# A hand-scheduled transformer block on one core: its written-out order replaced by another one

## The chip, the cores and the metric

The kernel runs on one core of a Trainium2 chip. The metric is the device time of one execution in microseconds (us). Five queues of instructions run at once and meet only through semaphores: PE (matmuls and their weight loads), ACT (activations), DVE (vector work), POOL (more vector work) and SP, which here only issues DMAs. Each queue is strictly in order: an instruction that waits holds everything behind it.

## The reference

One sequence of S = 2048 rows of D = 448, in bf16; 16 heads of 28; a gated feed-forward of F = 1792. Cut to what matters:

```python
q, k, v = layernorm(x) @ wqkv                       # 16 heads of 28
pq, pk  = q @ w_phi, k @ w_phi                      # per head, 28 x 28
phi_q   = concat(softmax(pq), softmax(-pq))         # 56 features; phi_k likewise
kv, z   = sum_s phi_k[s] v[s]^T, sum_s phi_k[s]     # over all 2048 rows
o       = (phi_q @ kv) / (phi_q @ z + 1e-6)
h       = x + o @ wo
out     = h + (sigmoid(hn @ w_gate) * (hn @ w_up)) @ w_down     # hn = layernorm(h)
```

The sum over s makes a point that all rows must pass: no output of attention exists before the last row's phi_k is summed.

## The kernel before, in words

The 2048 rows are 16 tiles of 128 (t = 0 to 15). All work is one list of about 1,000 tasks, `K.list`, in `build`. A task names its engine, the tasks it needs, the PSUM banks it may take, and an estimated duration (`dur`), landing time (`lat`) and DMA size. The string `PLAN` (line 31) is the order: each item is a task's number in the list; `.4-7` gives it PSUM banks 4 and 7; `~` moves it to its other engine. `planned` (line 113) reads the string, `emit` (line 147) gives each engine its queue in that order and adds the waits. The estimates are not read there: they served whoever searched the order, and reach the chip only through the string. Tasks with `lock=True` on DVE and the POOL task next to them in the string are made to wait for each other (line 126), so that they don't run at once.

The tasks that matter here, with the line of their instruction:

- **First half, until `kvz`.** Per pair of tiles PE projects k and v (`kp`, `vp`, line 513). Per tile t: two exponentials on ACT into `ek` (`ekp`, `ekm`, line 598; three buffers), the sum of each head on DVE (`ss`, line 611) and its reciprocal (`rs`, line 614), the product `phi` on POOL (line 618; DVE for tiles 12, 14 and 15), v scaled on ACT (`v1`, line 603), and `kv` on PE (line 631), which adds the tile to one PSUM bank. Between these DVE computes the layernorm statistics (`bst`, `agg`, lines 532 and 534) and POOL the factors (`ve`, `pow`, `neg`, lines 540 to 544). `kvz` (DVE, line 695) takes the finished sum.
- **Queries.** `qp` on PE, two exponentials on ACT (line 653), half sums `hs` on POOL (line 667), `sq` and `rq0` on DVE (lines 670, 672), `rq` and `em` on POOL (lines 674, 680; `em` of some tiles on DVE), then a DMA transpose `eT` on SP (line 688).
- **Output of attention, per tile.** `num` on PE (line 704), `rd` and `o` on DVE (lines 712, 714), the transpose `oT` (PE and ACT for tiles 0 and 1, a DMA transpose for each later pair, line 735), `wo_` on PE, `h`, `bst2`, `agg2` on DVE (lines 768 to 773), `ve2`, `pow2`, `nb` on POOL (lines 774 to 787), `hn` on ACT or DVE (lines 783 to 791), and the transpose `hT` (PE for tiles 0 and 1, a DMA transpose after that, line 809).
- **Feed-forward, in five chunks of 2, 4, 4, 4 and 2 tiles.** `gu` (line 513): gate and up products for 14 blocks of columns; each pair of blocks needs four PSUM banks. The chunk's first `gu` needs `hT` of all its tiles. `tg` on ACT (tanh, line 844) and `hh` on DVE (line 851) free the banks. `dn` (line 870) is the down product of one tile, `fin` (line 877) adds it to h, `st` (line 879) stores it. `gu1` below is the chunk of tiles 2 to 5, `gu2` that of tiles 6 to 9, `gu3` of 10 to 13, `gu4` of 14 and 15.
- **Fillers.** `dm` (line 813) multiplies constants and keeps PE busy while it would wait.
- **SP.** All loads, DMA transposes and stores are issued by the one queue SP, in the order of the string.

Of the kernel before, what the change touches and what calls it, by code (L numbers as in the profile page):

```python
# [10 lines left out]
P = 128  # L11
# [20 lines left out]
58 59 60 61 22 661.0-0 67.0-0 20 68 64.1-1 65 69 66 73.2-2 74 70.3-3 75 9 13 15 44 10 62 63 167.4-4 165.5-5 94.6-6  # L32
91.7-7 120 71 72 97.0-0 88.1-1 89 98 95 92 118 121 21 4 119 168~ 5 122 123 124 99~ 96~ 166 90 93 112.2-2 113 125 127
114 128 115 126 169.3-3 171 173 175 170.5-5 76.4-4 172 174 176 193.0-1 177.6-7 180 179 182 77 186 187 183 189 136
190 137 138 132 134 133 139 135 116 129 130 131 184 191 117 140 141 195.2-3 178 78 181 194 196 197 185.4-4 198 188
204 199 205 206 211.5-6 85.0-0 200 82.7-7 212 213.1-2 192 214 83 201 207 86 142 202 208 149 215 216 87 79.3-3
229.0-5 203 84 217 222 224 223 218 150 80 219 143 147 145 144 148 146 209 220 151 152 81 231.1-7 230 234 233 232
247.2-6 240 241 225 226 227 103.3-3 106.0-0 210 221 242 235 248 104 105 249.5-7 109.1-1 107 228 110 100.3-3 101 250
153 251 252 236 156 237 238 243 157 244 254 158 255 160 154 161 155 159 245 102 111 253 108 265.2-3 266 239 319.1-5
258 259 270 269 256 261 262 162 163 263 164 272 277 276 279 273 246 662.0-0 257 320 274 321 322 328 260 327 323 280  # L40
281 267.0-6 283.2-3 284 268 301.1-7 287 288 271 264 335.2-5 302 294 295 278 305 306 329 324 330 331 325 290 297 291
332 292~ 298 326 51 45 46 54 52 334 333 47 336 285.0-3 275 344 345 282 303.1-6 286 304 308 312 313 315 309 316 289
370.5-7 293 299 310~ 307 338 296 314 337 353.0-1 371 354 300 311 379 363 362 380 355 356 373 372 317~ 318 455 346
339 347 421.3-6 461.2-2 456.1-1 422 515.4-4 462 348 463 457 340 458 364 349 350 357 341 365 366 358 464.7-7 387.0-2
519.5-5 459.1-1 465 520 431 460 521 423 430 522 424 342 367 343 352 351 55 516 543 544 545 517 537 546 538 388
404.1-7 518 396 389 390 539 469.6-6 547.5-5 359 470 540 405 541.3-3 466.4-4 397 406 414 407 413 548~ 542~ 663.0-0
701.0-5 702.2-3 703 704 705 707 360 368 361~ 467 471 468 374 381 709.1-6 710.4-7 711 712 375 708 706 715 713 382 716
376 714 383 717.2-3 718.0-5 719 720 721 369 664.4-4 476.4-4 473.7-7 723 722 724 477 474 472 56 725.1-6 726.2-3 727
728 523.0-5 524 478 475 391 398 384 377 385 378 729 731 392 399 393 400 730 733.4-7 734.1-6 735 736 739 737 408 549
732 550 551 409 740 557 479 525.0-2 526 573 558 741.1-3 742.5-6 743 744 386 401 394 395 402 552 425 553 554 415 403  # L50
565 738 559 560 561 562 566 555 747 745 567 568 569 570 749.0-2 750.4-7 751 752 563 753 571 746 748 755 574 483.1-1
438.3-5 480.6-6 575 484 485 754 576 439 481 756 577 578 556 564 572 487.1-1 490.0-0 760.2-2 579~ 491 482 426 488 489
492 580 763.4-7 764.1-6 765 766 447 440 441 448 767 769 761 416 432 433 449 450 451 770 768 410 442 411 486 527.3-5
493 529.0-2 528 530 771.1-6 772.4-7 773 774 605 589 606 581 597 777 775 779.2-5 780.0-3 781 782 598 590 417 607 591
776 582 434 599 778 427 785 786 428 412 452 418 592 783 443 444 583 784 787.1-6 788.4-7 789 790 419 429 435 608 609
# [166 lines left out]
def build(nc, A_x, A_wqkv, A_w_phi, A_wo, B_w_gate, B_w_up, B_w_down, out):  # L222
# [16 lines left out]
    with ExitStack() as es:  # L239
# [67 lines left out]
        def TS(t):  # L307
            return slice(t * P, (t + 1) * P)
# [335 lines left out]
        for u in range(NT // 2):  # L644
# [39 lines left out]
            for a, n in ((t0, 1), (t1, 1)) if u < 2 else ((t0, 2),):  # L684
                for t in range(a, a + n):
                    ET[t] = ("eT", a)
                w = a % NEQ
                task(("eT", a), "sp", 1.25 if n == 1 else 1.9, lambda e, a=a, n=n, w=w: e.dma_start_transpose(
                    out=eqT[:, a:a + n, :, :].rearrange("p t k s -> p (t k) s"),
                    in_=eq[:, w:w + n, :, :].rearrange("p t k s -> p (t k s)")),  # L690
                    [("em", t) for t in range(a, a + n)], lat=1.1, kind="tr", size=1.42 * n)
# [8 lines left out]
        for t in range(NT):  # L700
# [18 lines left out]
            if n == 1:  # L719
                def f(e, t=t):  # L720
                    for k in range(4):
                        r = e.matmul(bank[got(("oP", t))[0]][:, k * P:k * P + P], lhsT=o_pad[:, t % 4, k * P:(k + 1) * P],
                                     rhs=ident[:], start=True, stop=True)
                    return r
                task(("oP", t), "pe", 0.26, f, [("o", t), "ident"], banks=ANY, until=[("oT", t)], mode=128)

                def f(e, t=t):
                    return e.copy(oT[:, t % 4, :, :].rearrange("p g s -> p (g s)"), bank[got(("oP", t))[0]])

                def f2(e, t=t):  # L730
                    return e.tensor_copy(oT[:, t % 4, :, :].rearrange("p g s -> p (g s)"), bank[got(("oP", t))[0]])
                task(("oT", t), "act", 0.53, f, [("oP", t)] + last_read, alt=("dve", 0.6, f2))
            elif t % 2:
                w = slice(t0 % 4, t0 % 4 + 2)
                task(("oT", t0), "sp", 1.25, lambda e, w=w: e.dma_start_transpose(
                    out=oT[:, w, :, :].rearrange("p t g s -> p (t g) s"),
                    in_=o_pad[:, w, :].rearrange("p t k -> p (t k)")),
                    [("o", t0), ("o", t)] + last_read, lat=1.1, kind="tr", size=1.42)
# [27 lines left out]
        for t in range(NT):  # L766
# [40 lines left out]
                task(("hT", t), "act", 0.48, f, [("hP", t)] + read, alt=("dve", 0.6, f2))  # L807
            else:
                task(("hT", t), "sp", 1.25, lambda e, t=t: e.dma_start_transpose(
                    out=hnT[:, :, TS(t)], in_=hn[:, t % NHN, :]), [("hn", t)] + read, lat=1.1, kind="tr", size=0.72)  # L810
# [109 lines left out]
```

## Time and profile before

| | us |
|---|---|
| three runs, median (lowest to highest) | 208.51 (208.28 to 208.68) |
| the profiled execution's own time | 209.01 |
| its span, first to last instruction | 207.3 |
| PE busy | 197.0 (95%) |
| DVE busy | 132.6 (64%) |
| ACT busy | 94.5 (46%) |
| POOL busy | 79.9 (39%) |

The profiled execution took 209.01 us, of which 207.3 us are the span that the profile shows and 1.7 us lie around it. The granted clock of PE is 1.00 over the whole span.

How to read it: a busy PE includes matmuls whose ends are modelled, so small losses between them don't show as idle time. The distance from the start of one task to the start of the next is the better measure. From the timeline of PE the tasks' own paces are (us): `kp`, `vp`, `qp` or `wo_` for two tiles 0.77 + 0.57; `gu` for two blocks of a 4-tile chunk 3.02, of a 2-tile chunk 1.53; `dn` 2.65; `num` 0.23; `kv` 0.24; a filler 0.43.

### The profile page before, as it was taken

How to read it: one execution, taken by the hardware profiler on the slowest of the kernel's cores; microseconds unless marked ns; L12 is line 12 of the kernel's file. 1: busy time of each engine (PE TensorE's matmuls, PEld its weight loads, DVE VectorE, ACT ScalarE, POOL GpSimd, SP SyncE). 2: the span in 40 equal slices, each digit the busy share in tenths (PEclk: the TensorE clock that was granted, in tenths of full speed). 3: DMA queues.
4: the chain of work that ended last, by engine and by line, in shares of the span. 5: the costliest groups of instructions: out<-in, count | busy, mean ns of one | idle time of the engine just before them, and what ended most of it. 6: DMA issues, size and time to landing. Idle time of an engine off the chain costs nothing.

```text
span 207.3 us, 4996 instructions
## 1 busy us (share of the span) xinstructions
PE 197.0 (95%) x2028; PEld 108.9 (53%) x2028; DVE 132.6 (64%) x306; ACT 94.5 (46%) x181; POOL 79.9 (39%) x142
## 2 busy tenths in 40 slices
PE   6799999999999897999999989999999999999995
PEld 2444544545486553555556434444554555897553
DVE  2799999898898896796533555569305535453222
ACT  3879999999971380232541023322110344442000
POOL 8559999859677853208900000101501000000000
PEclk9999999999999999999999999999999999999999
DMA  5999999450787958003692400500134020000014
GB/s 155 234 277 201 293 302 368 169 115 0 159 143 131 213 80 128 0 3 69 133 150 52 101 0 0 106 0 2 28 73 136 3 52 0 3 3 0 0 50 130
DMA packets 49751, 21.06 MB, mean 102 GB/s; under 512 B 40512, under 2 KB 48704, under 8 KB 49728
## 3 DMA queue, kind: packets, MB, share of 16 engines
q1 hardware_dynamic: 49584, 20.71, 45.3%
q8 instruction: 16, 0.26, 0.5%
q14 instruction: 7, 0.06, 0.1%
q10 hardware_dynamic: 144, 0.03, 0.1%
HBM read 9.20 MB, written 1.84 MB: 53 GB/s over the span
## 4 chain that ended last, share of the span: by engine, by line
PE 51%; DMA 13%; ACT 13%; DVE 11%; POOL 5%; SPq 3%; issue 2%; DVEq 0%; POOLq 0%; ACTq 0%
PE ps L513 38%; PE ps L870 12%; ACT hh L598 4%; DMA oT<-o_pad 4%; DMA xT<-hn 4%; ACT eq L653 3%; ACT hh L603 3%; DMA x_sb<-in_A_x_dram 3%; POOL hh L618 2%; DMA eqT<-eq 2%; SPq L357 2%; DVE st L771 2%; DVE o_pad L714 2%; DVE x_sb L768 2%; DVE hh L851 1%
## 5 line engine op out<-in xcount | busy, mean ns | idle before, releaser
L513 PE MATMUL ps<-xT,wg_sb 64*128 64x512 bf16 (+1 forms) x490 | 87.2, 333 | 3.1 <-DMA xT<-hn 1.8
L513 PE MATMUL ps<-xT,wu_sb 64*128 64x512 bf16 (+1 forms) x490 | 87.1, 333 | 0.0
L844 ACT ACTIVATE tg<-ps 128x512 f32<-128x512 f32 (+1 forms) x70 | 33.6, 512 | 73.4 <-PE ps L513 71.0
L851 DVE SCALAR_TENSOR_TENSOR hh<-tg,ps 128x512 bf16<-128x512 f32 (+1 forms) x70 | 38.5, 575 | 31.3 <-ACT tg L844 31.2
L513 PEld LDWEIGHTS ps<-xT,wg_sb 64*128 64x128 bf16 x490 | 45.4, 94 | 23.7 <-issue 3.4
L513 PEld LDWEIGHTS ps<-xT,wu_sb 64*128 64x128 bf16 x490 | 45.3, 94 | 14.1
L870 PE MATMUL ps<-wd_sb,hh 128*128 128x448 bf16 (+2 forms) x252 | 43.6, 332 | 0.1
L870 PEld LDWEIGHTS ps<-wd_sb,hh 128*128 128x128 bf16 x252 | 22.9, 98 | 18.9 <-DVE mv L773 0.4
L618 POOL TENSOR_TENSOR hh<-hh,rsum 128x896 bf16<-128x896 bf16 x13 | 21.8, 1699 | 0.0
L877 DVE SCALAR_TENSOR_TENSOR x_sb<-ps,x_sb 128x448 bf16<-128x448 f32 (+2 forms) x18 | 9.7, 560 | 18.8 <-PE ps L870 18.7
L774 POOL TENSOR_SCALAR rs<-mv 128x1 f32<-128x1 f32 x14 | 2.7, 192 | 49.2 <-DVE mv L773 48.5
L598 ACT ACTIVATE hh<-ps,rs 128x448 bf16<-128x448 f32 x32 | 18.9, 662 | 0.6 <-PE ps L584 0.3
L653 ACT ACTIVATE eq<-ps,rs 128x448 bf16<-128x448 f32 x32 | 18.2, 678 | 0.0
L611 DVE TENSOR_REDUCE ssum<-hh 128x32 f32<-128x896 bf16 x16 | 16.8, 1054 | 0.8 <-ACT hh L598 0.7
L667 POOL TENSOR_TENSOR halves<-eq 128x448 f32<-128x448 bf16 x14 | 13.4, 972 | 9.9 <-DVE sq L670 6.4
L680 POOL TENSOR_TENSOR eq<-eq,rq 128x448 bf16<-128x448 bf16 x15 | 14.0, 941 | 1.7 <-PE ps L513 1.4
L789 ACT ACTIVATE hn<-x_sb,nb,rs 128x512 bf16<-128x512 bf16 x9 | 7.2, 812 | 15.7 <-DMA xT<-hn 9.0
L513 PE MATMUL ps<-Wq,xT 64*128 64x448 bf16 x112 | 12.8, 351 | 0.1
L513 PE MATMUL ps<-Wvc,xT 64*128 64x448 bf16 x112 | 12.6, 350 | 0.2
L513 PE MATMUL ps<-Wk,xT 64*128 64x448 bf16 x98 | 11.6, 351 | 0.2
L513 PE MATMUL ps<-wo_sb,oT 64*128 64x448 bf16 x98 | 10.6, 350 | 0.4 <-DMA oT<-o_pad 0.3
L714 DVE TENSOR_TENSOR o_pad<-ps,rden 128x448 bf16<-128x448 f32 x16 | 9.3, 603 | 2.2 <-DMA oT<-o_pad 2.1
(103 smaller groups left out, 188.4 us busy)
## 6 DMA issues: line engine op xcount, KB each, us to landing
wg_sb<-in_B_w_gate_dram SPq DMA_DIRECT2D x2, 896.0 KB, 5.8
wu_sb<-in_B_w_up_dram SPq DMA_DIRECT2D x2, 896.0 KB, 9.5
out_dram<-x_sb SPq DMA_DIRECT2D x14, 112.0 KB, 1.8
x_sb<-in_A_x_dram SPq DMA_DIRECT2D x3, 448.0 KB, 5.9
wd_sb<-in_B_w_down_dram SPq DMA_DIRECT2D x3, 448.0 KB, 6.7
hh<-in_A_wqkv_dram SPq DMA_DIRECT2D x4, 196.0 KB, 4.1
wo_sb<-in_A_wo_dram SPq DMA_DIRECT2D x2, 336.0 KB, 8.1
x_sb<-in_A_x_dram SPq DMA_DIRECT2D x2, 224.0 KB, 4.3
```

The source lines that it names most:

```text
L513: r = e.matmul(ap(), lhsT=st(blk, rows), rhs=mv(blk, rows), start=first and i == 0, stop=not first and i == 2, tile_position=(rows.start, 0))
L598: task((key, t), "act", 0.53, lambda e, t=t, s=s, i=i, b=kb: e.activation(signs(ek[:, s, :])[:, :, :, i, :], heads2(bank[b()][:, 0:D]), AC ...
L611: task(("ss", t), "dve", 1.0, lambda e, s=s: e.tensor_reduce(ssum[:, s, :], ek[:, s, :].rearrange("p (h d) -> p h d", d=DH), AX.X, ALU.add ...
L618: return e.tensor_tensor(phi[:, t % NPHI, :, 0:GP].rearrange("p k (a d) -> p k a d", d=DH), ek[:, s, :].rearrange("p (k a d) -> p k a d", ...
L653: task((key, t), "act", 0.53, lambda e, w=w, t=t, i=i, b=bk[j]: e.activation(signs4(eq[:, w, :, 0:GP])[:, :, :, i, :], heads2(bank[b()][:, ...
L667: task(("hs", t), "pool", 0.9, lambda e, w=w, half_=half_, by4=by4: e.tensor_tensor(half_, by4(eq[:, w, :, 0:GP])[:, :, :, 0:DH // 2], by4 ...
L680: return e.tensor_tensor(ap, ap, rq[:, w, :].rearrange("p (k h) -> p k h", h=2)[:, :, :, None].to_broadcast([P, NPAIR, 2, DH]), ALU.mult)
L714: task(("o", t), "dve", 0.56, lambda e, t=t, res=res: e.tensor_tensor(o_pad[:, t % 4, 64 * (t % 2):64 * (t % 2) + D].rearrange("p (h d) -> ...
L844: task(("tg", c, f_), "act", 0.51 if n == 4 else 0.3, lambda e, j=j, N=N, b=gb[i]: e.activation(tg[:, j % NSG, 0:N], bank[b()][:, 0:N], AC ...
L851: e.scalar_tensor_tensor(hhT[c % 2][:, f_, 0:N], tg[:, j % NSG, 0:N], 1.0, bank[b()][:, 0:N], op0=ALU.add, op1=ALU.mult), deps)
L870: r = e.matmul(bank[b][:, cols], lhsT=hhT[c % 2][:, f_, ts], rhs=wd_sb[:, f_, cols], start=(f_ == 0), stop=(f_ == FT - 1))
L877: e.scalar_tensor_tensor(X(t)[:, cols], bank[got(first)[0]][:, cols], 0.5, X(t)[:, cols], op0=ALU.mult, op1=ALU.add), [nm, ("hn", t)])
```

## The change

The string `PLAN` is another order of the same tasks. Beside it, estimates are changed that only the search reads:

```diff
-load("wv0", ..., 0.6)                 +load("wv0", ..., 0.7)          (wv1 too)
-task(("eT", a), "sp", ..., lat=1.1)   +lat=1.6 if a < 6 else 2.6
-task(("oT", t0), "sp", ..., lat=1.1)  +lat=1.7 if t < 6 else 2.6
-task(("hT", t), "sp", ..., lat=1.1)   +lat=1.6 if t < 6 else 2.8
```

No task is added or removed but one filler (five in place of four). These tasks change engine: `em` 5 and 10 from POOL to DVE, `em` 4 from DVE to POOL; `hn` 5 and 15 from DVE to ACT, `hn` 11 from ACT to DVE; `hT` 1 from DVE to ACT; and in the first 10 us `W2` 0 and 1, `WTc` 0 from ACT to DVE, `W2` 3 and `xTc` 1 from DVE to ACT.

The first line of the string, for its look:

```diff
-16 17 8 23 24 25 26 27 28 29 30 31 32 33 34 35 36 37 0 18 3 19 1 7 43 11 53 38 39 50 40 41 42 49 48 2 12 14 6 57.7-7
+8 16 17 11 9 14 43 10 1 0 23 24 25 26 27 28 29 30 31 32 33 34 35 44 36 37 38 39 40 41 42 52 56 50 51 46 3 18 4 19 45
...
```

Resolved to the engines' queues, the places that the prediction speaks of are these (- before, + after; tasks left out are "..."; rq0_0 is DVE's `rq0` of tile 0, pow2_1 is `pow2` of tile 1, and rq1, em5, hn1 are `rq`, `em`, `hn` of tiles 1, 5, 1).

```diff
 DVE, around the last rows of keys
-ss12 ss13 rs12 phi12 rs13 ss14 ss15 rs14 rs15 phi14 phi15 kvz
+ss12 sq0 rs12 rq0_0 phi12 ss13 rs13 ss14 ss15 rs14 rs15 phi14 phi15 kvz
 POOL, the same
-phi11 rq1 rq0 em1 em0 phi13 hs3 hs2 hs5 ...
+phi11 rq1 rq0 em1 em0 phi13 hs3 hs2 hs5 ...      (rq0, not em0, is what waits for phi12)
 POOL, before gu0
-em2 pow2_1 pow2_0 rq4 em5 hs6
+em2 rq4 rq5 em4 pow2_1 pow2_0 hs6
 DVE, before gu0
-bst2_1 agg2_1 ve2_1 bst2_0 agg2_0 hn1 ve2_0 rq0_4 rd3 hn0 hT1 hT0 em4 rd2 o3 o2
+bst2_1 bst2_0 agg2_0 agg2_1 em5 ve2_1 ve2_0 rd3 hn1 hn0 o3 hT0 rd2 o2
 PE, from gu0 to gu1 (each gu0 is one of its seven pairs of blocks)
-gu0 gu0 gu0 dm num5 num4 gu0 wo_1 gu0 wo_2 gu0 gu0 num7 qp7 num6 num8 num9 dn1 gu1
+gu0 num5 num4 gu0 gu0 wo_1 gu0 wo_2 gu0 gu0 qp7 gu0 num9 num6 num8 num7 dn1 gu1
 PE, from gu1 to gu2
-gu1 (all) with wo_3 wo_4, num11 dn0 num13 dn3 num12 num15 num14 dn4 num10 dn5 gu2
+gu1 (all) with wo_3 wo_4, dn0 num10 num11 num13 dn3 num15 dn4 dn5 num14 wo_5 num12 gu2
 PE, from gu2 to gu3
-gu2, wo_5, gu2 ..., wo_6 wo_7, gu2, dn2 dn6 dn8 dn9 dn7 gu3
+gu2 ..., wo_6, gu2 ..., wo_7, dn2 dn6 dn9 dn7 dn8 (end of wo_7) gu3
 SP, loads
-... x8 wd0 xT8 wg1 x12 xT12 wg0 wo3 wu0 wo0 wo1 wd1 wu1 eT1 eT0 wo2 eT3 eT2 wd2 eT4 oT2 wd3 oT4
+... x8 xT8 x12 xT12 wu1 wd3 wg1 wu0 wo1 wo0 wd2 wo2 wo3 eT1 eT0 wd1 wd0 wg0 eT3 eT2 eT4 oT2 oT4
 SP, later
-eT10 eT12 st1 eT14 hT7 hT6 hT9 hT8 oT10 st5 oT14 oT12 hT11 hT12 hT10 st3 hT13
+st1 eT10 eT12 eT14 hT6 st0 oT10 hT9 hT8 hT7 oT12 oT14 hT10 st4 hT11 hT12 st2 st3 hT13
```

More of the change, by code (lines that the diff above doesn't have):

```diff
@@ L36 @@
[L36 to L55, printed above, removed]
@@ new lines @@
+6 55 47 48 57.7-7 58 59 60 61 661.0-0 70.0-0 71 67.1-1 118 2 15 12 13 64.2-2 73.3-3 68 20 119 65 74 22 72 69 66~ 75
+120 21 165.4-4 167.5-5 62 63 662.0-0 91.6-6 92 94.7-7 95 88.0-0 89 97.1-1 98 121 93~ 7 122 123 124 5 90~ 96~ 166 99
+168 112.2-2 113 127 125 114 115 128 126 169.3-3 171 173 175 79.4-4 170.6-6 172 174 193.0-1 176 177.5-7 178 194
+76.2-2 180 179 182 80 183 116 129 117 130 184 131 186 187 189 136 190 138 134 132 135 137 133 139 191 81 195.3-6 181
+188 185.4-4 196 204 197 198 205 206 199 211.5-7 192 229.0-1 212 85.6-6 140 141 142 200 77 78 201 207 86 216 215 87
@@ new lines @@
+208 149 202 223 222 82.3-3 230 213.2-5 203 209 218 83 219 220 225 145 226 147 143 146 148 150 144 227 151 152 153 84
+214 217 224 234 231.6-7 210 100.3-3 101 232 233 235 103.2-2 104 247.0-5 221 102 240 241 109.6-6 248 105 251 252 236
+160 237 238 243 158 244 161 254 255 154 156 159 155 157 245 249.1-3 110 106.2-2 107 228 108 250 111 259 253 242 258
+265.0-2 239 266 270 269 319.1-6 320 246 256 162 163 261 262 272 327 328 276 277 322 321 329 273 257 263 283.5-7
+267.0-6 284 164 287 288 274 279 330 280 290 323 281 331 291 324 268 301.1-2 260 302 335.3-5 264 271 295 278 294 305
@@ new lines @@
+306 292~ 325 332 326 334 333 663.0-0 285.0-6 336 286 303.1-7 275 312 289 313 338 282 293 304 353.0-2 297 298 299 345
+314 337 344 296 307 515.7-7 354 421.3-5 300 362 356 363 355 308 315 309 316 310~ 317~ 311 318 422 455 519.6-6
+461.1-1 370.0-2 456.4-4 346 347 339 364 462 348 340 463 457 341 458 349 357 342 350 54 53 49 352 358 365 359 366 343
+351 371 464.1-1 459.4-4 423 430 424 465 460 520 521 516 517 537 543 372 431 522 373 380 379 404.1-3 387.5-6 518 388
+389 469.4-4 360 367 361 368~ 544 538 369 545 539 470 546 540 405 547.0-0 541.2-2 466.7-7 471 374 381 390 407 548 396
@@ new lines @@
+406 542~ 664.5-5 665.5-5 701.4-5 702.0-2 703 704 705 707 413 414 397 467 468 382 375 706 476.1-1 473.7-7 708 477 474
+478 475 709.4-5 710.0-2 711 712 717.1-3 718.6-7 719 720 391 398 376 383 713 715 714 723 721 472 479 523.4-5 524 384
+377 385 378 392 399 400 393 716 722 725.0-2 726.1-3 727 728 729 549 557 731 550 724 525.4-5 526 551 732 558 559 565
+730 573 733.6-7 734.1-3 735 736 394 401 402 395 408 560 552 553 554 561 566 562 386 403 737 738 567 568 741.0-2
+742.4-5 743 744 739 555 563 569 574 740 575 747 570 745 571 748 576 415 746 556 564 438.6-7 749.1-3 750.4-5 751 752
@@ new lines @@
+753 755 577 578 754 756 416 439 490.0-0 480.2-2 487.1-1 483.3-3 760.4-4 481 491 492 484 485 482 432 409 761 433 488
+434 489 410 579 572 580 763.0-5 764.2-3 765 766 440 448 447 441 769 767 771.6-7 772.1-4 773 774 425 435 449 426 427
+417 428 436 411 450 770 418 451 452 442 775 768 777 412~ 443 444 778 776 779.2-3 780.0-5 781 782 785 783 786 486 493
+527.1-4 787.6-7 788.0-5 789 790 784 793 791 794 792 529.2-3 528 530 795.0-5 796.6-7 797 798 589 581 597 799 801 598
+605 582 583 606 802 800 599 803.1-4 804.2-3 805 806 807 809 811.6-7 812.0-5 813 814 607 590 808 815 817 816 810 818
@@ new lines @@
+591 757.1-1 419 762 420 494.4-4 758 495 429 584 437 445 496 497.6-6 504.7-7 505 498 499 453 600 446 608 609 610 601
+602 585 454 586 587 588 611 603 822.2-2 823 759 500 592 593 594 511.3-3 595 825.0-0 506 828.5-5 508.1-1 531.4-6
+501.2-2 826 512 513 502 829 532 621 613 503 509 510 612 604 596 831.0-7 832.3-5 833 834 835 837 836 614 838 839.4-6
+840.1-2 841 842 843 845 847.0-7 848.3-5 849 850 844 853 851 846 615 616 617 618 622 623 619~ 624 625 626 852 854
+855.4-6 856.1-2 857 858 859 861 862 507 514 620 827 860 533.0-7 863.3-5 864.1-2 865 866 867 534 868 627~ 628 869 637
@@ new lines @@
+629 870 871.4-6 872.3-5 873 874 877 878 875 879.0-7 880.1-2 881 882 535.3-5 638 630 876 639 631 632 633 640 634 883
+885 819.4-4 886 884 635~ 887.6-6 896.1-1 890.2-2 893.0-0 820 641 642 888 891 536 894 645 646 647 653 897 636 821 824
+643 644 899.4-7 900.2-6 901 902 903 905 907.0-3 908.1-5 909 910 904 906 654 913 911 655 914 912 915.4-7 916.2-6 917
+918 921 922 919 920 648 656 649 657 650 658 923.1-5 924.0-3 925 926 929 930 931.2-6 932.4-7 933 934 927 651~ 928 659
+935 937 652 830 660 939.0-3 940.1-5 941 942 938 936 943 945 944 946 947.4-7 948.2-6 949 950 951 953 952 954 967.0-3
@@ L71 @@
+968.1-5 969 970 973 971 975.4-7 976.2-6 977 978 972 974 979 981 980 982 983.0-3 984.1-5 985 986 989 987 990 988
+991.4-7 992.2-6 993 994 999.1-5 1000.0-3 1001 1002 995 997 998 996 1007.2-6 1008.4-7 1009 1010 1005 1003 1004 1006
+1015.1-5 1016.0-3 1017 1018 1011 1012 1013 1019 1021 955.2-2 1022 956 1014 1023.6-6 958.0-0 961.3-3 1031.2-2 1020
+962 1035.4-4 1036 1032 1033 959 964.7-7 965 1024 895 889 1034 892 898 957 963 960 966 1025 1026 1027.1-1 1037 1038
+1028 1029 1030
 """
@@ L389, in build @@
         load("phk", wphK[:], phi_v.rearrange("(b p) j -> p b j", p=GP), 1.0)
-        load("wv0", Wv[:, 0:2, :], wv_v[0:256, :].rearrange("(b p) n -> p b n", p=P), 0.6)
-        load("wv1", Wv[:, 2:4, :], wv_v[192:448, :].rearrange("(b p) n -> p b n", p=P), 0.6)
+        load("wv0", Wv[:, 0:2, :], wv_v[0:256, :].rearrange("(b p) n -> p b n", p=P), 0.7)
+        load("wv1", Wv[:, 2:4, :], wv_v[192:448, :].rearrange("(b p) n -> p b n", p=P), 0.7)
         load_w(0)
@@ L690, in build @@
                     in_=eq[:, w:w + n, :, :].rearrange("p t k s -> p (t k s)")),
-                    [("em", t) for t in range(a, a + n)], lat=1.1, kind="tr", size=1.42 * n)
+                    [("em", t) for t in range(a, a + n)], lat=1.6 if a < 6 else 2.6, kind="tr", size=1.42 * n)
         Q_OF = {t: ("qp", t // 2, 1) for t in range(NT)}
@@ L809, in build @@
                 task(("hT", t), "sp", 1.25, lambda e, t=t: e.dma_start_transpose(
-                    out=hnT[:, :, TS(t)], in_=hn[:, t % NHN, :]), [("hn", t)] + read, lat=1.1, kind="tr", size=0.72)
+                    out=hnT[:, :, TS(t)], in_=hn[:, t % NHN, :]), [("hn", t)] + read, lat=1.6 if t < 6 else 2.8, kind="tr", size=0.72)
         for i in range(40):
```

21 lines of the change are left out of this document (1 added, 20 removed).

## The prediction

> **What bounds the kernel now.** I read the page first, then the chain of waits, then the timelines of PE, POOL, DVE and SP at the places where the chain leaves PE.
>
> ```profile
> span 207.3 us, 4996 instructions
> ...
> PE   6799999999999897999999989999999999999995
> ...
> DVE  2799999898898896796533555569305535453222
> ACT  3879999999971380232541023322110344442000
> POOL 8559999859677853208900000101501000000000
> ...
> q8 instruction: 16, 0.26, 0.5%
> ```
>
> The reader is to see two halves. A slice is 5.2 us. From slice 3 to slice 11 (to about 57 us) PE, DVE and ACT are all full and POOL nearly; after that PE alone is. So the first half is a race of four engines to `kvz` and to the first `gu`, and the second half is PE's own work plus the places where a transpose comes late. Those places stand in the chain:
>
> ```profile
> 76.93 3.44 DMA xT<-hn
> ...
> 80.51 23.98 PE ps L513 x224
> ...
> 114.89 4.86 DMA oT<-o_pad
> ...
> 154.35 2.42 DMA xT<-hn
> ...
> 156.91 32.03 PE ps L513 x392
> ```
>
> Three times PE waits for a DMA transpose: for `hT5` before `gu1`, for `oT10` (which frees the buffer of a later `o`, and that a PSUM bank) in `gu2`, for `hT13` before `gu3`. From 156.91 on nothing but PE. PE's timeline gives the idle times in brackets (1.33 and 0.84 here, 0.45 at 156.91):
>
> ```profile
> 80.51 0.37 PE L513 MATMUL ps<-xT,wg_sb 64*128 64x512 bf16 x1 [1.33 <-DMA xT<-hn]
> ```
>
> ```profile
> 120.53 0.39 PE L513 MATMUL ps<-xT,wg_sb 64*128 64x512 bf16 x1 [0.84 <-DVE o_pad L714]
> ```
>
> Measured from start to start against the tasks' usual paces, these three cost 1.5, 1.3 (another 0.13 of idle time follows at 121.70) and 0.6 us. Between 57.1 and 76 PE loses 2.5 us more in small waits and a filler. PE's work is the same in both orders, so the change is worth what it does to these waits, plus what it does to the first half.
>
> **Step A, up to `kvz` (47.30 us): no change.** In the new order DVE no longer has `ss13` (pace 0.97) ahead of `phi12`, but POOL has `em1` and `rq0` (0.90 + 0.20) behind `phi12`, where now only `em0` is. From there the links are the old ones: `em0`, `phi13`, `phi14`, `phi15`, `kv`, `kvz`. That is 1.10 - 0.97 = +0.1; I take 0. Bounds: DVE's idle gaps in this stretch add up to 1.1 us, which an order that fits better could win (-1.1). On the other side, statistics `bst` (0.53) stand between a sum and its reciprocal for tiles 1, 5, 6 and 7, and each may hold POOL's next `phi`: three more than bearable would be +1.6. The moved loads don't reach this step: the two loads that leave their place before and behind `xT8` let x of tiles 12 to 15 land earlier. `wg0` now goes out behind `eT0`, at about 46; the rows of such loads have 5.8 to 9.5 us to landing, so 56 at the latest, before the first `gu` needs it.
>
> **Step B, first `gu`: 57.10 becomes 58.4.** This is what now holds it, in POOL's and DVE's timelines:
>
> ```profile
> 54.75 0.56 POOL L776 TENSOR_TENSOR rs<-rs,neghalf 128x1 f32<-128x1 f32 x1 [0.59 <-DVE rs L774]
> 55.84 0.22 POOL L674 TENSOR_TENSOR rq<-rq,sq 128x16 f32<-128x16 f32 x1 [0.53 <-DVE hn L783]
> 56.02 0.94 POOL L680 TENSOR_TENSOR eq<-eq,rq 128x448 bf16<-128x448 bf16 x1
> ```
>
> `pow2` of tile 0 (line 776) runs first, `rq4` and `em5` after it. The change puts `rq4`, `rq5` and `em4` ahead of `pow2` on POOL (0.2 + 0.2 + 0.9), and `em5` (0.62) on DVE ahead of `ve2`. POOL ends `em2` at 53.17 today; plus 1.3 that is 54.5, `em5` to 55.1, `ve2` and two `pow2` to 56.4, `hn1` and `hn0` (0.36 apart, both now after both `pow2`) to 57.2, instead of 55.76. That is +1.4; POOL has waits of 0.1 to 0.3 before it that I expect to close, so +1.3. Bounds: +0.6 if all of POOL's waits close, +2.0 if `em5` waits for a busy DVE. The fillers before this `gu` cost nothing while it waits; if it doesn't wait they cost 0.43 each.
>
> **Step C, from the first `gu` to `gu1`: 80.51 becomes 79.8.** PE's work between them is 7 x 1.53 (`gu`) + 2 x 1.34 (`wo_`) + 1.34 (`qp7`) + 6 x 0.23 (`num`) + 2.65 (`dn1`) = 18.8 us, so PE could be there at 58.4 + 18.8 = 77.2. What decides is `hT5`, and its chain begins with `eT4`:
>
> ```profile
> 57.64 2.98 SPq L688 DMA_TRANSPOSE eqT<-eq  x1
> ...
> 64.59 1.24 SPq L735 DMA_TRANSPOSE oT<-o_pad  x1
> ...
> 71.56 6.84 SPq L809 DMA_TRANSPOSE xT<-hn  x4
> ```
>
> `eT4` leaves at 55.1, when `em5` ends, not at 57.64. It landed 4.95 us after its issue: 60.1. The new order has one pair of `gu` first (to 59.9), then `num5` and `num4` to 60.6; DVE has two `hh` (0.38 each), two `rd` and two `o` (0.25, 0.55 each) to 62.8, against 64.56 today. `oT4` leaves at 62.9 (64.59) and lands after its 3.65 at 66.5. `wo_2` stands behind four pairs and `wo_1` and ends at 68.4 (70.02). From there to `agg2` of tile 5 DVE takes 4.3 us today; with two `hh` in other places I take 4.5: 72.9. POOL needs `ve2`, `hs11`, `pow2`, `nb` (0.2 + 0.97 + 0.55 + 0.27, 0.1 between): 75.1. `hn5`, now on ACT, takes 0.82 instead of 0.41: `hT5` leaves at 76.0. The landings of line 809 run from 2.4 to 4.2 us, so 78.4 to 80.2.
>
> The row that says which: while `hT3` and `hT4` were under way, the DMA view of 76 to 78 us shows (queue, packets, MB, share; and issues with us to landing)
>
> ```profile
> q8 instruction: 1, 0.02, 2.9%
> q14 instruction: 1, 0.01, 2.6%
> ...
> xT<-hn SPq DMA_TRANSPOSE x2, 3.8
> ```
>
> Two fetches of instructions (q8, q14) lie in these 2 us, and the two transposes took 3.8 where the median is 2.5. The page has 16 fetches of q8 for PE's 4056 matmuls and weight loads, one for some 250 of them. Counted in the new order the same fetch falls on the `num` just ahead of `dn1`, at about 77, beside `hT5`. So I take 3.8: `hT5` lands at 79.8, and `gu1` is 0.7 earlier than now.
>
> [...]
>
> **Step D, after `gu1`: -1.9.** (1) From `gu1` to the end of `dn0` is 7 x 3.02 + 2 x 1.34 + 2.65 = 26.5, so 106.3. `num10` and `num11` follow at once (now `num10` stands behind `dn4`); `fin0`, three `rd`, two `o` on DVE take 2.3, `oT10` leaves at 108.8 and with today's 4.86 lands at 113.7. `gu2` starts 37.1 after `gu1`, at 116.9, and needs that `o` at 117.8: the 1.3 go. What may be late next is `hT7`, now behind `st0`, `oT10`, `hT9` and `hT8` in SP's queue, at 1.25 each: it leaves at 112.6 to 113.8, and lands by 116.3, or at 4.2 by 118.0. That is up to 1.1 of a new wait against 116.9; I take none, by the median of 2.5. (2) `wo_6` and `wo_7` start some 10 us of PE's work earlier before `gu3` than now, and `hT13` has only two stores ahead of it: at least 5 us of room, the 0.6 go. The end of the kernel has the same last `dn`, `fin` and store.
>
> **The sum.** A 0, B and C together -0.7, D -1.9: -2.6 us. The span goes from 207.3 to 204.7, the profiled execution's 209.01 to 206.4. The median of the runs is 0.5 below that execution, so 208.51 becomes **205.9 us**.
>
> **Rivals.**
> - *`hT5` lands as fast as the median* (2.5; no fetch beside it): 78.5 instead of 79.8, another -1.3: 204.6. For it: the fetch's place is counted, not seen. Against it: three of the four `hT` here took 3.4 or more. 0.13.
> - *The gain before `gu1` is lost, that behind it stays*: `hT5` or `hT7` at 4.2 and over, or A at +1: 80.5 to 81.5 for `gu1`, so -1.9 to -0.9: about 207.1. 0.20.
> - *The order only moves the waits*: A's +1.2, B's +2.0 and `hT7` late by 0.5 eat the 1.9: within 0.2%, 208.4. 0.08.
> - *Slower: the first half runs late.* Everything from `kvz` to `gu1` hangs on one chain, so a microsecond at `kvz` is one at the end. DVE is full there, and in the new order `bst`, `sq0` and `sq1` (0.53, 1.0, 1.0) stand ahead of the reciprocals that POOL's `phi` wait for. Held up by 0.5 at eight of the sixteen tiles, `kvz` is 4 later: 209.9. It decides from 2.6 us on, `kvz` at 49.9. For it: DVE's and POOL's full digits. Against it: about as many such tasks stand in the same places now. 0.17.
>
> **How the numbers follow.** My forecast (206.6 to 205.2) has 0.42. About 0.2% (0.4 us) is what a measurement of this kernel can tell from no change. Faster by more: 0.42 + 0.13 + 0.20 = 0.75; same 0.08; slower 0.17. The range takes in the first rival and A's lower bound (204.3) and the slower case up to 0.8 over today's time (209.3); outside are some 0.05 below and 0.13 above.
>
> **What would show it.** `kvz` within 1 us of 47.3; the first `gu` about a microsecond later than 57.1, behind `em4` and `em5`; `eT4` issued before 56; `gu1` at 79 to 80.5 and behind it no idle time of PE over 0.3 in `gu2` and before `gu3`. Wrong would be: `kvz` after 49, a wait of PE for `hT7` before `gu2`, or the first `gu` on time.

## The result and the profile after

| | before | after |
|---|---|---|
| median, 4 runs each (lowest to highest) | 208.44 us (208.28 to 208.68) | 206.31 us (206.24 to 206.78) |
| the profiled execution, its span | 209.01, 207.3 | 206.24, 204.5 |
| first `gu` | 57.10 | 57.98 |
| `gu1` | 80.51 | 78.54 |
| `gu2` | 116.50, then a wait of 0.84 | 116.06, no wait |
| `gu3` | 156.91 | 153.32 |
| end of the last `dn` | 205.00 | 201.40 |
| from there to the end of the span | 2.3 | 3.1 |

The ratio of the times is 0.990 (95% interval 0.988 to 0.992): 2.1 us faster, where 2.6 were predicted; the profiled executions differ by 2.8. Lines have moved down by one in the changed kernel. The page after:

```profile
span 204.5 us, 5003 instructions
...
PE   7899999999999998999999999999999999999993
...
DVE  2999999898799979729574466465128345543033
ACT  3789999998983580423342042423002443551000
POOL 8569999768759865600830003003000300000000
```

Of PE's three dips of before (8, 7 and 8; counting from 0, slices 13, 15 and 23) one 8 is left, in slice 15, and its last digit has gone from 5 to 3: at the end PE is idle for longer. The chain of waits after (start, us, what):

```profile
57.98 1.71 PE ps L514 x28
...
77.89 0.63 DVE x_sb L878
...
78.54 23.98 PE ps L514 x224
...
115.56 23.91 PE ps L514 x224
...
152.81 32.52 PE ps L514 x398
```

No transpose is named any more. That is not quite true at 78.54, as PE's timeline shows:

```profile
78.54 0.37 PE L514 MATMUL ps<-xT,wg_sb 64*128 64x512 bf16 x1 [0.69 <-DVE x_sb L878]
```

`gu1` doesn't need `fin` of tile 1 (line 878); it ended at 78.51 only by chance. `hT5` landed at 78.29, and in all twelve runs below `gu1` starts 0.24 to 0.25 after that landing, wherever `fin1` ends. In some of them the view names the landing (run e7):

```profile
79.31 0.37 PE L516 MATMUL ps<-xT,wg_sb 64*128 64x512 bf16 x1 [0.92 <-DMA xT<-hn]
```

The issues of the transposes in SP's timeline, to be held against 57.64, 64.59 and 71.56 before:

```profile
54.58 1.95 SPq L689 DMA_TRANSPOSE eqT<-eq  x1
...
61.95 1.24 SPq L736 DMA_TRANSPOSE oT<-o_pad  x1
...
70.86 5.73 SPq L810 DMA_TRANSPOSE xT<-hn  x4
```

What the prediction had left out stands at the end. SP's timeline after, two of the last nine stores, and DVE's last three `fin`:

```profile
199.62 0.33 SPq L880 DMA_DIRECT2D out_dram<-x_sb  x1
...
202.51 0.40 SPq L880 DMA_DIRECT2D out_dram<-x_sb  x1
```

```profile
200.75 0.96 DVE L878 SCALAR_TENSOR_TENSOR x_sb<-ps,x_sb 128x336 bf16<-128x336 f32 x3 [0.37 <-PE ps L871]
```

The last `fin` ends at 201.71, but its store `stb14` goes out at 202.51: SP is busy with older stores. `sta15` (197.64, it waits for `fina15`) stands ahead of `st7`, `st9`, `st10` and `st12`, whose data are older, `st7`'s from 150.8 on. Then the queue stands for 1.18 us ahead of 199.62: before the eleventh store `emit` makes SP wait for all 24 loads and 12 transpose semaphores, all long reached. Seven stores follow back to back, some 0.5 us each. Before, `stb14` went out right behind its `fin` (205.04 to 205.32):

```profile
205.34 0.33 SPq L879 DMA_DIRECT2D out_dram<-x_sb  x1
```

The kernel before has the same block of waits at the same count of stores (1.17 us, to 201.11), but there it ends 3.9 us before the last `fin` starts; after the change it ends only 1.8 us before (199.62 and 201.44). One of the 18 stores, `stb15`, goes out on ACT's queue and not on SP's.

### The profile page after: what moved, and what is told of

Same layout as the page of the kernel before. It is cut to its first block, busy times and chain, and to the rows that moved or that the text cites. A ratio compares the mean times of both kernels' runs of the same rounds, so it can differ in the third digit from the quotient of the medians.

```text
span 204.5 us, 5003 instructions
## 1 busy us (share of the span) xinstructions
PE 196.8 (96%) x2029; PEld 106.5 (52%) x2029; DVE 132.7 (65%) x306; ACT 96.0 (47%) x182; POOL 79.0 (39%) x141
## 4 chain that ended last, share of the span: by engine, by line
PE 76%; ACT 7%; DVE 6%; POOL 5%; issue 2%; DMA 2%; SPq 1%; DVEq 0%; POOLq 0%; ACTq 0%
PE ps L514 51%; PE ps L871 21%; POOL hh L619 3%; ACT eq L654 2%; ACT hh L599 2%; DVE ssum L612 2%; DMA wphK<-in_A_w_phi_dram 2%; PE ps L705 1%; DVE hh L619 1%; POOL rs L543 1%; DVE x_sb L878 1%; PE ps L585 1%; SPq L358 1%; DVE sq L671 1%; PE ps L475 1%
## 5 line engine op out<-in xcount | busy, mean ns | idle before, releaser
L514 PE MATMUL ps<-Wvc,xT 64*128 64x448 bf16 x112 | 13.2, 351 | 0.2
L681 POOL TENSOR_TENSOR eq<-eq,rq 128x448 bf16<-128x448 bf16 x14 | 13.0, 942 | 1.0 <-DVE eq L681 0.8
L514 PE MATMUL ps<-wo_sb,oT 64*128 64x448 bf16 x98 | 11.3, 350 | 0.1
L790 ACT ACTIVATE hn<-x_sb,nb,rs 128x512 bf16<-128x512 bf16 x10 | 7.8, 810 | 5.5 <-POOL nb L788 3.0
L715 DVE TENSOR_TENSOR o_pad<-ps,rden 128x448 bf16<-128x448 f32 x16 | 9.8, 620 | 0.2
```

The lines of the kernel that those rows point to most:

```text
L514: r = e.matmul(ap(), lhsT=st(blk, rows), rhs=mv(blk, rows), start=first and i == 0, stop=not first and i == 2, tile_position=(rows.start, 0))
L681: return e.tensor_tensor(ap, ap, rq[:, w, :].rearrange("p (k h) -> p k h", h=2)[:, :, :, None].to_broadcast([P, NPAIR, 2, DH]), ALU.mult)
L715: task(("o", t), "dve", 0.56, lambda e, t=t, res=res: e.tensor_tensor(o_pad[:, t % 4, 64 * (t % 2):64 * (t % 2) + D].rearrange("p (h d) -> ...
```

## The experiments

Each is the changed kernel with one edit (e10: three), timed beside the kernel before on the same chip, whose median was 208.5, 208.6 and 208.5 in the three sets of runs. Ratios are to that; the change itself was timed by itself, so runs of one set are best held against each other. Executions differ in when the first transpose `eT1` goes out (41.77 after; 41.55 to 42.35 in the runs that don't touch PE's start), so "net" times are counted from `eT1`'s issue, and put on the scale of the changed kernel (41.77). e3 and e4 turned out to be repeats of the change (below): they have `gu1` 0.3 later and 0.1 earlier, so a difference of 0.2 or 0.3 in the last column says nothing.

| run | median us | ratio (95%) | net change of `gu1` |
|---|---|---|---|
| the change itself | 206.31 | 0.990 (0.988 to 0.992) | |
| e1_tail | 205.77 | 0.987 (0.985 to 0.990) | -0.1 |
| e2_em_late | 213.69 | 1.025 (1.023 to 1.028) | +7.2 |
| e3_pe_nops | 206.67 | 0.991 (0.989 to 0.994) | +0.3 |
| e4_dve_nops | 206.67 | 0.991 (0.988 to 0.993) | -0.1 |
| e5_pe_small | 208.22 | 0.998 (0.995 to 1.001) | +0.8 |
| e6_dve_small | 206.18 | 0.989 (0.986 to 0.991) | 0.0 |
| e7_eT4_late | 206.60 | 0.990 (0.988 to 0.993) | +0.2 |
| e8_em_behind | 213.05 | 1.022 (1.018 to 1.025) | +4.0 |
| e9_pe_pieces | 206.84 | 0.993 (0.991 to 0.995) | 0.0 |
| e10_all | 206.26 | 0.990 (0.988 to 0.993) | +0.2 |
| e11_rd3_late | 206.62 | 0.992 (0.990 to 0.995) | +0.2 |
| e12_num10_late | 207.91 | 0.997 (0.996 to 0.999) | 0.0 |

**The end.**

```diff
 SP, last stores
-st8 st6 sta15 st7 st9 st10 st12 st11 st13 sta14 stb14
+st8 st6 st7 st9 st10 st12 sta15 st11 st13 sta14 stb14
```

> The changed kernel with the stores of tiles 7, 9, 10 and 12 put ahead of the first half store of tile 15 on SP's queue; nothing else moves. Main theory: in the changed kernel the end is bound by SP's queue of stores (7 stores back to back behind a gap of 1.2 us, the last one issued 0.8 us after its data was ready). Then the last store goes out at 201.8 instead of 202.5, the span falls from 204.5 to about 203.7 and the time by 0.8, to about 205.5 us. Rival: the end is bound by the last landings or by what follows them, whatever the queue does: span 204.4 to 204.6, time 206.2 to 206.4.

205.77, against 206.67 in two repeats of the change timed with it (e3, e4, below): -0.9, and none of e1's six executions (205.27 to 205.97) is slower than the fastest of those twelve (205.97). In e1's SP and DVE timelines the store is right behind its `fin` again:

```profile
201.48 0.35 SPq L880 DMA_DIRECT2D out_dram<-x_sb  x1
```

```profile
200.49 0.96 DVE L878 SCALAR_TENSOR_TENSOR x_sb<-ps,x_sb 128x336 bf16<-128x336 f32 x3 [0.37 <-PE ps L871]
```

From the last `fin` to the end of the span: 2.0 before, 2.8 after, 2.0 here (203.5 - 201.45). The main theory holds. The edit moves the late store and the block of waits together (the block now stands ahead of `st10`, and `sta15` behind it), so how the 0.8 is shared between the two is not shown. This kernel has the lowest median of all in the table; the interval of its ratio overlaps with that of e6.

**Step B and `eT4`.** Three runs bear on whether the early `em4` and `em5` cost the first `gu`, and buy `gu1`.

```diff
 e2: POOL  -rq4 rq5 em4 pow2_1 pow2_0 hs6 hs7        +pow2_1 pow2_0 hs6 hs7 rq4 rq5 em4
     DVE   -em5 ve2_1 ve2_0 rd3 hn1 hn0 o3 hT0       +ve2_1 ve2_0 rd3 hn1 hn0 o3 hT0 em5
 e8: POOL  +pow2_1 pow2_0 rq4 rq5 em4 hs6 hs7        DVE  +ve2_1 ve2_0 hn1 hn0 rd3 o3 hT0 em5
 e11: DVE  -em5 ve2_1 ve2_0 rd3 hn1 hn0              +em5 ve2_1 ve2_0 hn1 hn0 rd3
```

> The changed kernel with rq4, rq5, em4 (POOL) and em5 (DVE) put back behind pow2, hn and hT of tiles 0 and 1; nothing else moves. Main theory (step B pays for step C): the first gu starts about 0.9 earlier, at 57.1, but eT4 is issued at 57 or later instead of 54.58, oT4 1.5 or more later, and gu1 is at 79.8 to 80.6 instead of 78.54; the time rises by 1.2 to 2 us, to 207.5 to 208.3. Rival (the chain through eT4 has slack, B was only a cost): gu1 comes with the first gu, at 77.6 to 78.0, and the time falls to 205.4 to 205.8.

> The changed kernel with step B undone: on POOL rq4, rq5 and em4 behind both pow2, on DVE em5 behind hT of tile 0, and rd3 behind hn of tile 0 (as in the kernel before). Main theory: hn0 starts at 55.3 to 55.6 instead of 56.11, the first gu at 57.1 to 57.6 instead of 57.98, but eT4 goes out at 58.0 to 58.4 instead of 54.58, and gu1 comes 3.5 to 5 later, at 82 to 83.5; the time rises by as much, to 210 to 211.5. Rival (B only costs): gu1 comes with the first gu, 0.4 to 0.9 earlier, and the time falls by as much.

> The changed kernel with rd3 behind both hn of tiles 0 and 1 on DVE (in the change it stands ahead of them and waits for num3, which PE has at 55.1 to 55.5); em4 and em5 stay ahead of pow2. If num3 through rd3 holds the first gu, hn0 starts at 55.4 to 55.6 instead of 56.11 and the first gu at 57.3 to 57.5. If em4 and em5 through pow2 hold it (my step B), pow2 of tile 0 still ends at 55.75, hn0 starts at 55.8 to 56.0, and the first gu comes at most 0.3 earlier, at 57.7 to 57.98. As num5 stands behind the first pair of gu and not behind eT4's landing (59.04), gu1 and the time follow the first gu by the same amount; rival: the landings near hT5 eat it, and the time stays within 0.2.

In both first runs `eT4` goes out much later, and everything behind it:

```profile
60.55 1.85 SPq L689 DMA_TRANSPOSE eqT<-eq  x1
```

```profile
59.17 2.96 SPq L689 DMA_TRANSPOSE eqT<-eq  x1
```

(e2, then e8.) Net they are 5.8 and 4.6 later, and `gu1` comes 7.2 and 4.0 later: the rivals fall. PE waits for `eT4`'s landing ahead of `num5`, 5.29 us in e2 and 3.04 in e8, and `num5` starts 5.2 and 3.9 later net. The other 2.0 of e2 are PE's clock, in its page (a slice is 5.3 us):

```profile
PE   7999999999927999899999999999999999999994
...
PEclk9999999999985999999999999999999999999999
```

PE stands still from 59.65 to 64.94; the record of the granted clock has one half from 62.11 to 68.93, and until then the matmuls run at half pace (a pair of 64x256 starts every 0.21 us, after that every 0.11). e8's profile, with the shorter wait, has a granted clock of 1.000, but it is of its fastest execution, 210.26; the others took 212.1 to 214.0 with a granted clock of 0.984 to 0.992, and e2's five all have 0.984. So the 213.69 and 213.05 of the table hold a loss of clock beside the late `eT4`, and 210.26 is nearer to what the transposes alone cost.

The first `gu` came hardly earlier in e2 (57.81 net, 57.98 after) and later in e8 (58.80), where both texts had it 0.4 to 0.9 earlier. In e2 I had put `em4` behind `hs6` and `hs7` too, later than in the kernel before, and `rd3`, which waits for PE's `num3`, stands ahead of `hn1`. In e8 the lock between POOL and DVE made `hn1` wait for `em4`, since `em4` now stood ahead of it in the string:

```profile
56.40 0.73 DVE L784 TENSOR_SCALAR hn<-x_sb,mv,rs 128x512 bf16<-128x512 bf16 x2 [2.43 <-POOL eq L681]
```

So neither isolates B. In the changed kernel both reasons show, POOL's `pow2` behind `em4` and `em5` (to 55.75) and `rd3` behind `num3` (`hn1` starts at 55.78):

```profile
54.64 1.11 POOL L777 TENSOR_TENSOR rs<-rs,neghalf 128x1 f32<-128x1 f32 x2 [0.80 <-DVE rs L775]
```

```profile
55.55 0.26 DVE L713 RECIPROCAL rden<-ps 128x16 f32<-128x16 f32 x1 [0.93 <-PE ps L705]
```

e11 parts them: with `rd3` out of the way DVE's `hn1` waits for POOL's `pow2`:

```profile
55.56 0.74 DVE L784 TENSOR_SCALAR hn<-x_sb,mv,rs 128x512 bf16<-128x512 bf16 x2 [1.16 <-POOL rs L777]
56.21 0.25 DVE L713 RECIPROCAL rden<-ps 128x16 f32<-128x16 f32 x1
```

Net, that is 55.78, the very time at which the changed kernel has it behind `rd3`. The two reasons lie side by side there, B's is enough, and the expected 0.3 didn't come: the first `gu` is 0.2 later net (58.22), since `rd3` now stands ahead of `hT0`. e2 shows `rd3`'s to be nearly enough too: without `em4` and `em5` ahead the first `gu` gained 0.17.

**Is `eT4` still on the path?**

```diff
 SP, ahead of eT4
+30 waits on a semaphore of POOL that has long been reached
```

> The changed kernel with 30 waits on a semaphore that has long been reached, on SP's queue right ahead of the issue of eT4: eT4 is issued 0.8 to 1.2 later than 54.58, nothing else changes place. Main theory (step C: the chain eT4, num5, o, oT4, wo_2, agg2, hn5, hT5 sets gu1): gu1 comes later by as much, at 79.3 to 79.8, and the time rises by 0.8 to 1.2. Rival (the chain through eT4 has slack, the gain of step C came from elsewhere): gu1 and the time stay within 0.3 of the changed kernel's.

The 30 waits took 0.78 us (26 ns each); `eT4` went out 0.78 later net. `num5` didn't move (59.65 net, 59.62 after), `oT4` neither, `gu1` by 0.2, no more than in a repeat. The rival holds: `eT4` now has 0.6 us of room, since `num5` stands behind the first pair of `gu`. e2 and e8 had used that room up.

**Step D.**

```diff
 PE  -dn0 num10 num11 num13 dn3 num15 dn4 dn5        +dn0 num11 num13 dn3 num15 dn4 num10 dn5
 DVE -fin0 rd10 ... o10 ... o11 fin3 o13 fin4        +fin0 ... o11 fin3 o13 rd10 o10 fin4
 SP  -hT6 st0 oT10 hT9 hT8 hT7                       +hT6 st0 hT9 hT8 hT7 oT10
```

> The changed kernel with a part of step D undone: num10 behind dn4 on PE, its rd and o behind o13 on DVE, oT10 behind hT7 on SP's queue; wo_5 stays ahead of gu2. Main theory (D's gain hangs on the early oT10): oT10 goes out at 112.8 to 113.5 instead of 107.71 and lands at 116 to 117.5 instead of 110.95; wo_5 waits for it, and o14, o15 as well; gu2 starts 1.5 to 3.5 later than 116.06 and the time rises by as much. Rival (oT10 had that much room, gu2's wait went for another reason, such as hT6 to hT9 landing earlier): gu2 within 0.3 of 116.06, the time within 0.2.

`oT10` went out at 112.52 and landed at 115.74, and PE stood still for it:

```profile
115.79 0.93 PE L514 MATMUL ps<-wo_sb,oT 64*128 64x448 bf16 x8 [1.37 <-DMA oT<-o_pad]
```

`gu2` came at 117.56 (+1.4 net), and the time is 1.3 us over e11's, timed with it (207.91 and 206.62). The main theory holds; the size is just below the expected 1.5, since `oT10` went out and landed (after 3.22) a little earlier than I had put it. The wait here is `wo_5`'s, which the kernel before had inside `gu2`: e12 shows that the new order lives on the early `oT10`, and doesn't bring back the old wait for the buffer of `o`.

**Fetches and landings.** Two runs were to move PE's and DVE's fetches by empty instructions, and three more by small real ones:

```diff
 e3: PE, ahead of each warm-up     +20 x nop
 e4: DVE, ahead of its first mW    +24 x nop
 e5: PE, warm-ups 2 to 4, first two fillers   -one matmul of 512 columns each   +12 to 14 matmuls of 1 column
 e6: DVE, ahead of its first mW    +20 memsets of 1 column
 e9: PE, warm-ups 1 to 4, first filler   -one matmul of 512 columns each   +16 matmuls of 32 columns
```

> The changed kernel with 100 empty instructions on PE's queue, 20 ahead of each of the five warm-up matmuls, where PE has no other work: PE's instruction fetches (q8) come some 100 instructions earlier from then on, the one at 74.4 at about 71. Main theory (a fetch makes a transpose that is under way land late): hT4 lands 2.4 to 2.6 after its issue instead of 4.28, and the late ones are now those under way at the new fetch times (eT8 or hT2 near 71); all other transposes of line 810 take 2.4 to 2.6. hT5, if it is only queued behind hT4, falls from 3.2 to 2.5 and gu1 from 78.54 to about 77.9, the time to about 205.7; if it is held by the q14 fetch at 76.5, it keeps 3.2 and the time stays within 0.2 of 206.3. Rival (long landings come from transposes that queue on each other): hT4 keeps 4.0 to 4.4, and the time stays.

> The changed kernel with 24 empty instructions on DVE's queue while DVE waits for its first transposes of weights (2.4 to 4.8 us). If the q14 fetch at 76.48 is DVE's, it comes some 24 DVE instructions earlier, near 68, and leaves hT4 and hT5: main theory then gives hT5 2.4 to 2.6 instead of 3.21 and hT4 the same 4.28 less at most 1, gu1 78.0, time about 205.8. If q14 at 76.48 belongs to another engine, it stays and so do hT5's 3.2 and the 206.3. Rival (fetches do nothing to landings): q14 moves, hT5 keeps 3.2, time 206.3.

No empty instruction is in the two traces, and the fetches stand within 0.6 us net of where they were: nothing shows that the empty instructions reached the chip. So e3 and e4 tell nothing of the theories; they are two repeats of the change (206.67 both). Even so their landings differ: `hT3` and `hT4` took 4.20 and 3.40 in e3, 2.42 and 4.29 in e4 (2.42 and 4.28 after), with the q8 fetch at 74.3 net in both.

> The changed kernel with three of the five warm-up matmuls and the first two fillers on PE (before 7 us) replaced by 64 matmuls of one column, so that PE has some 118 instructions more ahead of everything else: every later fetch of PE's queue (q8) comes some 118 of 256 instructions earlier, the one at 74.4 at about 70 to 71. Main theory (a fetch makes the transposes under way land late): hT3, hT4 and hT5 land 2.4 to 2.6 after their issue (hT4 4.28 now, hT5 3.21 now unless the q14 fetch at 76.5 holds it), gu1 comes up to 0.7 earlier than 78.54, and eT8 or hT2, under way near 70.5, land later than now (4.33 and 2.42). The time falls by 0 to 0.7. Rival (long landings come from transposes that queue on each other): hT4 keeps 4.0 to 4.4 and the time stays within 0.3 of the changed kernel's.

> The changed kernel with 20 memsets of one column on DVE while it waits for its first matmul (2.4 to 4.8 us). Both traces have a q14 fetch when DVE stands at its instruction 192 to 194 (76.48 in the changed kernel); if that fetch is DVE's, it comes 20 DVE instructions earlier, near 68. Main theory: hT5 then falls from 3.21 towards 2.5 (but not below what hT4, still beside the q8 fetch, leaves), gu1 comes 0.2 to 0.7 earlier and the time falls by as much. If the fetch stays at 76.5, it isn't DVE's; if it moves and hT5 keeps 3.2, then hT5 is late because hT4 is, and q14 has no part in it; the time stays within 0.2.

> The changed kernel with four of the five warm-up matmuls and the first filler on PE, 512 columns each, cut into 16 pieces of 32 columns: the same columns, but 75 matmuls (150 instructions with their weight loads) more, all before 5 us. Every later q8 fetch comes some 150 of 256 instructions earlier: the one at 74.4 near 69.5, the one at 65.7 near 62. Unlike the run with matmuls of one column, the start keeps its pace (kvz within 0.5 of 47.02). Main theory (a fetch makes the transposes under way land late): hT3, hT4 and hT5 land 2.4 to 2.6 after their issue, hT5 at 77.5 instead of 78.29, gu1 at 77.7 to 78.0 and the time falls by 0.5 to 0.8; if the fetch near 62 falls beside oT4, that lands after 4 instead of 3.08, wo_2 and all behind it come up to 1 later, and the gain is lost. Rival (long landings come from transposes that queue on each other): hT4 keeps over 4 and gu1 its place; the time stays within 0.2.

The 256 instructions to a q8 fetch in two of these texts fit the changed kernel's trace as a mean: PE has 2029 matmuls, 2029 weight loads and 49 other instructions for 16 fetches, 257 for one.

e5: the fetches moved, and the late landings with them. `hT3` and `hT4` took 2.42 and 2.45 (4.28 for `hT4` before the edit); `hT2`, now beside the fetch at 74, took 3.12, `oT4` beside one at 66 took 4.11 (3.08), `oT8` beside one at 84 took 4.32 (3.08). But everything came late, `kvz` by 2.6, for a reason of its own (last section). e6: the q14 fetch went from 76.5 to 62, so it is DVE's; `hT5` itself then took 2.41, but landed at the same net time (78.30, 78.29 after), because `hT4`'s issue held SP for 2.38 us. e9: `kvz` kept its place (47.02 net), the fetch of 74.4 came at 71.4 net (not 69.5). The DMA view of the changed kernel, 73.4 to 78.4, has both fetches beside `hT4` and `hT5`:

```profile
q8 instruction: 1, 0.02, 1.4%
q14 instruction: 1, 0.01, 0.4%
...
xT<-hn SPq DMA_TRANSPOSE x2, 3.7
```

The one of e9, 74.8 to 77.3, has no q8, and the issues of `hT4` and `hT5` beside it landed after 2.6 in the median:

```profile
q14 instruction: 1, 0.01, 1.3%
...
xT<-hn SPq DMA_TRANSPOSE x2, 2.6
```

`hT4` took 2.47, as expected; `eT8` and `hT2`, beside the fetch now, took 6.28 and 3.07 (4.33 and 2.42 after). But `gu1` stayed at 78.54 net: the delay was handed on. `hT2` held SP for 1.97 instead of 1.19, so `hT3`, `hT4` and `hT5` went out later, `hT5` at 75.5 net instead of 75.08, and `hT5`, beside the q14 fetch, took 2.8. Both theories have a part in these runs: `hT4` took 4.28 beside the fetch of 74.4 and 2.47 without it, and through the queue of transposes `hT2`'s longer hold made the last issue, `hT5`'s, 0.4 later. The gain of 0.5 to 0.8 didn't come (206.84, a ratio of 0.993).

**All together.** e1, e9 and e11 in one kernel.

> The changed kernel with three edits together: the warm-up matmuls in pieces, the four stores ahead of the first half store of tile 15, and rd3 behind hn of tile 0 on DVE. Main theory: the gains add: 0.7 to 0.9 at the end, 0 to 0.8 at gu1 through hT5, 0 to 0.3 through the first gu: 1.0 to 1.9 less than the changed kernel, a ratio to the kernel before of 0.981 to 0.986. Rival (one of the two edits of the first half makes another transpose late and only the end's gain is left): 0.7 to 0.9 less, a ratio of 0.986 to 0.988.

206.26: 0.4 less than e11 and 0.6 less than e9, timed with it, and the end is the short one (2.1 from the last `fin`). But the ratio, 0.990, is that of the change itself: neither text has it right, and what the end saves is lost before. In its profile `eT1` goes out 1.2 later than after, more than in any run without the pieces on PE, and 0.6 later in e9; whether the pieces cost this at the start stays open. e1 alone has the lower ratio (0.987), though the intervals overlap.

## Why the prediction was right, and where it wasn't

| step | predicted | measured |
|---|---|---|
| A, `kvz` | 0 | -0.28 |
| B, first `gu` (with A) | +1.3 | +0.88 |
| C, `gu1` (with A and B) | -0.7 | -1.97 |
| D, after `gu1` | -1.9 | -1.63 |
| the end | 0 | +0.8 |
| span | -2.6 | -2.8 |

- **A** right within its bounds; it was not tried apart.
- **B** right in kind and nearly in size: from `kvz` to the first `gu` the change costs 1.16 (9.80 before, 10.96 after), the rest is A. e11 shows `pow2` to be enough for the whole delay; that `em4` and `em5` are what makes it late is read from the timelines, as no run took both reasons away. That `rd3` waits for `num3` at the same time was not in the prediction.
- **C** right in direction, 1.26 too small (A and B included), so that `gu1`, at 78.54, lies before the 79 to 80.5 that were to show the prediction right. The mis-sized terms: DVE from the end of `wo_2` to `agg2` of tile 5 took 3.40, not the 4.5 I had put on the 4.3 of before, as `bst2` and `agg2` of tile 3 no longer stand between (-1.1); `hT5` landed after 3.21, not 3.8 (-0.6); POOL took 2.64, not 2.2 (+0.4); the rest is under 0.3 each. "Its chain begins with `eT4`" is only half right: `eT4` had to come early (e2, e8), but once it does it has room (e7), and PE's order, DVE and POOL lead to `hT5` (read from the timelines). `oT4` landed after 3.08, not 3.65.
- **D** right: no wait in `gu2`, none before `gu3`; `oT10` left at 107.71 (108.8) and landed at 110.95 (113.7). e12 shows that it must be early. D is 0.27 short, since PE took 37.5 from `gu1` to `gu2` and not 37.1, without a wait that the trace shows. `hT7` landed at 114.11, 1.9 before it was needed; the risk taken at nothing was nothing. The part with `hT13` (landed at 146.86 for `gu3` at 153.32) is read from the trace and not tried.
- **The end** is the step that failed: "The end of the kernel has the same last `dn`, `fin` and store." The three are the same, the queue ahead of the store is not. I had listed SP's order only up to `hT13`. e1 shows the 0.8.
- The fetch beside `hT5` was there, but its q8 part fell at 74.4, beside `hT4`; `hT5` was late by the queue. The first rival (2.5 for `hT5`) came true in e6 as to the landing (2.41) and not as to the time: `hT5` had left 0.8 later, behind `hT4`.

The total is right because C's 1.26 on the one side and D's 0.27 and the end's 0.8 on the other nearly cancel. That it came within 0.2 of the span is luck; the steps and their directions are not, but for the end.

## What to carry to other kernels

Follow each in-order queue to its last instruction, that of the stores too: one store whose data come late, put ahead of four that are ready, and a block of waits at a place where it can't be hidden cost 0.8 us together, and moving them took it back. When a transfer is brought forward, ask what stands beside it afterwards: `eT4` was worth microseconds (4.6 later, `gu1` 4.0 later in e8) until PE's order bound in its place, and then nothing more (0.78 later, `gu1` within 0.2 in e7). When an experiment makes PE stand for microseconds, look at its granted clock before the time is put down to the wait alone (e2: a stop of 5.29 us, and 6.8 us at one half). A delay that is moved along a queue of transposes is not removed (e9: `hT4` 1.8 faster, `gu1` at 78.54 net as before).

## What the runs showed of the hardware that was not expected

- **Instruction fetches and DMA transposes.** Over the 14 profiles, by the start and end of each fetch in the traces: of 108 transposes `hT` with no fetch in flight none took over 2.56 us (median 2.43); of 54 with a q8 fetch in flight 42 took over 2.8, up to 4.64 (median of the 54: 3.4); of 34 with a q14 fetch alone 3 took over 2.8, up to 3.33. The 14 kernels are nearly one kernel, so the same few transposes come again; that the late ones change with the fetch is what e5, e6 and e9 add. Where the fetch began less than 0.2 us before the usual end of `hT3`'s landing, it took 2.42 (after and in e4); where the fetch began 0.22 before, 4.20 (e3).
- **PE kept half its pace until 13.3 us in e5.** There, 14 matmuls of 112 columns from 7.6 us on take 1.46 us, in the changed kernel 0.85:

```profile
7.56 1.46 PE L481 MATMUL ps<-PhiK,hh 112*128 112x112 bf16 x14
```

```profile
7.46 0.85 PE L475 MATMUL ps<-PhiK,hh 112*128 112x112 bf16 x14
```

  From start to start that is 93 ns and 49 ns each, and e5 keeps the slow pace until 13.3 us. The views give a granted clock of 1.00 there in both, but the clock's own record begins only where the pace doubles: at 13.3 in e5, at 5.0 in the changed kernel, at 4.5 in e9, with pieces of 32 columns. The first warm-up matmul is at 1.51 in all three. In the ten profiles that have the changed kernel's own start on PE, the record begins at 4.2 to 7.5, 2.7 to 6.0 us after the first warm-up. e5, with 64 matmuls of one column, 27 ns apart, in place of three warm-ups and two fillers, lies far outside, 11.8 after it; what in its start makes the record late is not shown.
- **The granted clock fell in one long stop of PE.** It fell to one half 2.5 us into e2's stop of 5.29 us, and stayed there for 6.8 us. In e8's profile a stop of 3.04 us left it at 1.000.
- **Waits took SP time even when they were met:** 26 ns each in e7 (30 in 0.78 us), and 1.18 us, 33 ns each, for the block of 36 ahead of the eleventh store.
